# Chunk-selected attention with a gated MLP: scores of four pairs with 128-row contractions, k and q turned by TensorE, a new order

## The chip, the cores and the metric

The kernel runs on one core of one Trainium2 chip. Its time is the device time of one execution in microseconds (us). The core has five engines that run their own instruction streams and wait for each other by semaphores: TensorE (PE, matmuls and transposes), VectorE (DVE), ScalarE (ACT), GpSimd (POOL) and SyncE (SP), which in this kernel only issues DMAs. All loads, stores and DMA transposes go through SP's one queue.

## The reference

q, k and v have the shape (4 batches, 8 heads, 768 positions, 64). For every query a bound on its score with each chunk of 32 keys is made from the chunk's minimum and maximum, the six chunks with the highest bound among those that are not in the future are kept, and softmax attention runs over their keys alone, causally. The result goes through a gated MLP whose gate mixes positions.

```python
ub = sum(max(q * k_min, q * k_max))          # per query and chunk of 32 keys
ub = where(causal, ub, -1e9)
top = argsort(ub)[..., -6:]
scores = q @ k.T / 8                         # outside top or in the future: -1e9
attn = softmax(scores); x = attn @ v         # (4, 768, 512) after joining heads
h = relu(x @ w_in); u, v = h[:512], h[512:]
v_s = w_spatial @ normalised(v) + b_spatial  # mixes the 768 positions
out = (u * v_s) @ w_out
```

## The kernel before

Work is cut into 16 pairs of heads (pair i is batch i // 4, heads 2(i % 4) and the next one). The four pairs of batch 0 run in halves of 384 positions (tags `0a`, `0b` ...), the others whole (tags `4` to `15`). All work is on 16-bit floats; only the accumulators, loads and stores are 32 bits wide.

**How the order is set.** Every operation is an `Op` with a name, the engines that it may run on with a planned cost, its readers and writers. Nothing in the loops sets the order in time: `plan.replay(ORDER)` reads a long table, found by a search offline, word by word. `sc12_0P:10` says: operation `sc12_0` next, on engine P (P is PE, D is DVE, A is ACT, G is POOL, S is SP), its new buffers are number 1 and 0 of their rings. Each engine runs its own words in this order. The sizes of the rings stand in `RINGS` (L144); four matmul buffers `gen` (one PSUM bank each) and two `sc` (two banks each) are shared by all of PE's work. The planned costs stand in the functions `t_dve`, `t_act`, `t_pool`, `t_pe` (L27 to L40) and in the `op` calls; they matter to the search and not to the replay.

**Preparing a pair** (`load`, `prep`). k, q and v of the pair are loaded in 32 bits (`ld_`, L469 to L488): for v, and for k and q of pairs outside `PE_T` (pairs 10 to 15), each row of 64 numbers is one run of 256 bytes; for pairs in `PE_T`, six neighbouring rows go to one partition. `c_k`, `c_q`, `c_v` cast them (on POOL, DVE or ACT). To bring the 64 dimensions of both heads onto the 128 partitions, pairs in `PE_T` use six PE transposes (`t_k`, `t_q`, L516) and a copy out of PSUM (`e_k`, `e_q`, through `copy`, L302 to L306), and the other pairs one DMA transpose of k and q together (`x_kq`, L524). The result is a tile `kqT`. Then come the chunk maxima and negated minima (`kmm0`, `kmm1`, L530, DVE), their copy into a block layout for two heads (`km0`, `km1`), the rectified q and -q (`rq0`, `rq1`, L544 to L548), and the bounds on PE (`ub`, L558: for each of six tiles of 128 queries two matmuls of 48 columns, relu(q) with the maxima and relu(-q) with the negated minima). DVE adds the causal term to the diagonal chunks (`ubm`, L567), finds the six highest (`max`, L581), compares (`sel`, L602 or L605); `grd` (L590) writes a guard column. PE transposes the selection (`tsel`, L616, three transposes for a pair) and `es` copies it to the tile `selT`.

**Scores** (`attend`). A whole pair has three groups (`WHOLE`, L247), each with strips of key tile times query tiles in two buffers. For each strip and head a matmul of 64 rows gives q·k (L658; the two heads lie in rows 0 to 63 and 64 to 127), and a matmul of 32 rows adds the mask (L671: the selection times `expand`, a matrix of -30000 over each chunk). `exp` (ACT, L693) makes the weights, `tri` (POOL, L704) cuts the diagonal, `av` (PE, L727) multiplies with v and a column of ones, `rec` and `nrm` (DVE) divide, and `xx` (DMA, L748) or `tx` and `ex` turn the result for the MLP.

**The MLP of a batch** (`mlp`, called when the four pairs of the batch are done, its operations spread through the next batch's). Six v projections (`v`), their relu (`rv`), statistics (`bn`, `ag`), 1/sigma by two ACT operations (`ln`, `rs`), the normalisation (`vn`, L808, DVE), six u projections (`u`, `ru`), the mixing of positions (`s`, L826), the gate (`g`, L830, DVE), a DMA transpose (`xg`, L847), the output projection (`o`, L855), its eviction (`eo`) and the store (`so`, L860). Weights are loaded, cast and, for w_spatial, turned by PE (`tws`, `ews`). `WARM` are matmuls without use ahead of the first data (`w0` to `w3`, L424).

## Time and profile before

| | |
|---|---|
| median of three runs | 205.67 us (204.78 to 205.95) |
| the profiled execution's own time | 205.87 us |
| its span, first to last instruction | 204.0 us |
| mean granted clock of PE | 0.988 |
| busy: PE, DVE, ACT, POOL | 190.9, 164.5, 145.8, 80.1 us |
| bytes moved by DMA | 38.28 MB in 86989 packets, 74416 of them under 512 B |

In the lines that follow, a line of instruction groups names the source line, the engine, the operation, output and input tiles, shapes and the count, then busy time and mean duration, then the engine's idle time ahead of them and what ended it. A row of stretches has the stretch and its length, then the busy time of PE, PEld (weight loads), DVE, ACT and POOL with their numbers of instructions, then PE's granted clock, the mean busy share of the 16 DMA engines, and GB/s. A row of the chain has start, length, and what ran; the chain goes back from the last instruction to whatever released each step. A row of the timeline has start, length, engine, line, operation, tiles and count, and in brackets the idle time before it and what ended it.

### The profile page before, as it was taken

How to read it: one execution, taken by the hardware profiler on the slowest of the kernel's cores; microseconds unless marked ns; L12 is line 12 of the kernel's file. 1: busy time of each engine (PE TensorE's matmuls, PEld its weight loads, DVE VectorE, ACT ScalarE, POOL GpSimd, SP SyncE). 2: the span in 40 equal slices, each digit the busy share in tenths (PEclk: the TensorE clock that was granted, in tenths of full speed). 3: DMA queues.
4: the chain of work that ended last, by engine and by line, in shares of the span. 5: the costliest groups of instructions: out<-in, count | busy, mean ns of one | idle time of the engine just before them, and what ended most of it. 6: DMA issues, size and time to landing. Idle time of an engine off the chain costs nothing.

```text
span 204.0 us, 5938 instructions
## 1 busy us (share of the span) xinstructions
PE 190.9 (94%) x2282; PEld 103.3 (51%) x2282; DVE 164.5 (81%) x523; ACT 145.8 (71%) x232; POOL 80.1 (39%) x167
## 2 busy tenths in 40 slices
PE   7899989999998999798999999999999999999991
PEld 2456646576564455454355554544455456444440
DVE  2699999999999999798499896979998418894352
ACT  4689989999999498746797986687884673344221
POOL 5377848785795455631304642101451121000000
PEclk9969999999999999999999999999999999999998
DMA  5999999989999599699999869999200570701844
GB/s 167 278 249 292 287 359 280 319 223 310 275 208 238 92 224 236 142 145 263 236 213 230 155 78 262 148 261 224 40 0 3 132 154 5 204 2 51 206 156 157
DMA packets 86989, 38.28 MB, mean 188 GB/s; under 512 B 74416, under 2 KB 81584, under 8 KB 86960
## 3 DMA queue, kind: packets, MB, share of 16 engines
q1 hardware_dynamic: 86960, 37.89, 79.4%
q8 instruction: 18, 0.29, 0.6%
q14 instruction: 11, 0.09, 0.1%
HBM read 24.38 MB, written 6.29 MB: 150 GB/s over the span
## 4 chain that ended last, share of the span: by engine, by line
PE 59%; DVE 20%; DMA 7%; POOL 7%; issue 4%; ACT 2%; POOLq 0%; DVEq 0%; ACTq 0%
PE gen L776 16%; PE gen L826 11%; PE gen L855 7%; PE gen L727 7%; PE sc L658 6%; DVE kmm L530 5%; PE sc L671 4%; DMA st<-in_q_dram 3%; POOL n L306 3%; DMA late<-late 2%; PE sc L424 2%; DMA out_dram<-late 2%; DVE max L581 2%; DVE vn L808 2%; PE gen L616 2%
## 5 line engine op out<-in xcount | busy, mean ns | idle before, releaser
L693 ACT ACTIVATE e<-sc 128x768 f16<-128x768 f32 (+1 forms) x96 | 83.2, 917 | 23.3 <-PE sc L671 22.4
L704 POOL TENSOR_SCALAR_AFFINE_SELECT e<-e 128x512 f16<-128x512 f16 (+1 forms) x44 | 28.6, 662 | 31.8 <-ACT e L693 30.0
L826 PE MATMUL gen<-vn,wsT 128*128 128x512 f16 x144 | 34.4, 380 | 0.0
L530 DVE TENSOR_REDUCE kmm<-kqT 128x24 f16<-128x768 f16 (+1 forms) x40 | 30.7, 780 | 0.4 <-ACT kqT L304 0.2
L658 PE MATMUL sc<-kqT 64*128 64x128 f16 (+2 forms) x344 | 27.4, 272 | 0.3 <-ACT e L693 0.3
L727 PE MATMUL gen<-vt,e 128*128 128x65 f16 x672 | 24.8, 193 | 0.5 <-DVE selT L306 0.3
L727 PEld LDWEIGHTS <-e 128*128 128x128 f16 x672 | 23.0, 97 | 4.5 <-issue 1.6
L855 PE MATMUL gen<-w_out,late 128*128 128x512 f16 x96 | 23.7, 379 | 1.2 <-DMA late<-late 1.2
L830 DVE SCALAR_TENSOR_TENSOR late<-gen,bcol,u 128x512 f16<-128x512 f32 x24 | 17.7, 745 | 7.8 <-PE gen L826 7.8
L826 PEld LDWEIGHTS <-wsT 128*128 128x128 f16 x144 | 12.9, 98 | 15.7 <-issue 2.6
L671 PE MATMUL sc<-selT,expand 32*128 32x128 f16 (+2 forms) x344 | 19.0, 273 | 0.2 <-DVE selT L306 0.2
L658 PEld LDWEIGHTS <-kqT 64*128 64x128 f16 x344 | 11.8, 94 | 13.5 <-issue 9.8
L304 ACT ACTIVATE kqT<-gen 128x384 f16<-128x384 f16 (+1 forms) x24 | 15.0, 640 | 3.9 <-PE gen L516 3.7
L794 DVE BATCH_NORM_STATS2 stats<-vraw 128x6 f32<-128x512 f32 x24 | 15.8, 679 | 0.8 <-ACT vraw L783 0.8
L783 ACT ACTIVATE vraw<-gen 128x512 f32<-128x512 f32 x19 | 11.0, 607 | 6.7 <-PE gen L776 6.7
L306 POOL COPY km<-kmm 64x48 f16<-64x48 f16 (+1 forms) x27 | 6.6, 248 | 23.3 <-DVE kmm L530 19.6
L304 ACT ACTIVATE late<-gen 128x512 f32<-128x512 f32 (+1 forms) x12 | 7.1, 598 | 11.4 <-PE gen L839 5.3
L306 DVE COPY late<-gen 128x512 f32<-128x512 f32 x14 | 9.4, 687 | 7.1 <-PE gen L855 5.5
L581 DVE MAX8 max<-gen 128x8 f32<-128x20 f32 (+4 forms) x160 | 14.8, 164 | 0.1
L306 POOL CAST n<-st 128x768 f16<-128x768 f32 x17 | 13.9, 832 | 2.1 <-DMA st<-in_q_dram 1.6
L776 PEld LDWEIGHTS <-early 128*128 128x128 f16 x96 | 9.0, 98 | 11.0 <-issue 0.8
L783 ACT ACTIVATE u<-gen 128x512 f16<-128x512 f32 x18 | 10.5, 601 | 5.5 <-PE gen L776 5.5
(102 smaller groups left out, 299.3 us busy)
## 6 DMA issues: line engine op xcount, KB each, us to landing
out_dram<-late SPq DMA_DIRECT2D x24, 256.0 KB, 2.6
st<-in_q_dram SPq DMA_DIRECT2D x12, 384.0 KB, 5.8
st<-in_k_dram SPq DMA_DIRECT2D x12, 384.0 KB, 5.4
st<-in_v_dram SPq DMA_DIRECT2D x12, 384.0 KB, 6.1
st<-in_moe_w_spatial_dram SPq DMA_DIRECT2D x6, 384.0 KB, 5.1
st<-in_moe_w_in_dram SPq DMA_DIRECT2D x8, 256.0 KB, 4.4
early<-in_k_dram SPq DMA_DIRECT2D x8, 192.0 KB, 3.4
early<-in_q_dram SPq DMA_DIRECT2D x8, 192.0 KB, 3.7
```

The costliest lines, as they stand in the source:

```text
L304: e.activation(out=out, in_=in_, func=Act.Copy)
L306: e.tensor_copy(out, in_)
L530: lambda e, m=m, f=f: e.tensor_reduce(kmm.t[:, m, 0:nch], kq.t[:, 0, s0:s0 + ns].rearrange("d (c j) -> d c j", j=CHUNK), axis=AX.X, op=f, ...
L658: e.matmul(sc[z].t[:, a:a + len(qs) * P].rearrange("p (t c) -> p t c", c=P), lhsT=kq.t[r, 0, t * P:(t + 1) * P], rhs=qv[r, qs[0]:qs[-1] + ...
L671: e.matmul(sc[z].t[:, a:a + len(qs) * P], lhsT=expand.t[r, t * P:(t + 1) * P], rhs=selT.t[r].rearrange("p z c -> p (z c)")[:, c0:c0 + len( ...
L693: e.activation(out=e_.t[:, z, :, 0:w], in_=x.t.rearrange("p (h c) -> p h c", h=2)[:, :, 0:w], func=Act.Exp, scale=scale)
L704: e.affine_select(out=d, in_=d, compare_op=Alu.is_ge, fill=0.0, base=0, channel_multiplier=-1, pattern=[[0, 2 * len(zs)], [1, P]])
L727: e.matmul(avv()[:, n, hi, :], lhsT=es[g].t[:, zz, hi, c:c + P], rhs=vt.t[:, t, hi, 0:D + 1], start=(t == 0), stop=(t == qi))
L776: e.matmul(acc.t, lhsT=x.t[:, ko, t * P:(t + 1) * P], rhs=w.t[:, ko, :], start=(ko == 0), stop=(ko == NDO - 1))
L783: e.activation(dst.t, acc.t, func=Act.Relu)
L826: e.matmul(acc.t, lhsT=wsT.t[:, s, t * P:(t + 1) * P], rhs=vn[s].t, start=(s == 0), stop=(s == NQT - 1))
L855: e.matmul(acc.t, lhsT=gT.t[:, a2 * KO + ko, :], rhs=w_out.t[:, ko, :], start=(ko == 0), stop=(ko == KO - 1))
```

## The change

- **Wide scores.** For pairs 12 to 15 (`WIDE`) one matmul of 128 rows replaces the two of 64 and 32. Its stationary tile `kw` has, for head 0, k in rows 0 to 63 and `expand` in rows 64 to 127, and for head 1 the other way round; k is copied there by `kw0` and `kw1`. Its moving tile `qw` has q and the selection of a head below each other: `c_s` copies q beside the selection in a tile `qs`, `sel` and `grd` write into the same tile, and the DMA transpose `xs` (SP) turns all of it. `tsel` and `es` of these pairs are gone.
- **Turning k and q.** `PE_T` is now pairs 0 to 11. In pairs 12 to 15 (`K_T`) k is turned by PE and loaded in the form of `PE_T`, and q by a DMA transpose of its own (`x_q`). `x_kq` and its ring `kq16` are gone.
- **Bounds.** In pairs 0 to 5 (`UB3`) the bound is three matmuls, q with the maxima, relu(-q) with the maxima, relu(-q) with the negated minima, so that `rq0` is gone, and the causal term is a fourth small matmul (`tri` with the new tile `first`), so that `ubm` is gone.
- **The normalisation** is scale and shift: a new small DVE operation `sh` makes -mean/sigma, and `vn` may run on ACT, which six of the 24 do.
- **Order, rings and planned costs.** `ORDER` is new throughout; `st` has 9 buffers, `n16` 6; the tiles lie in a different order in memory, after a tile of 64 columns that nothing uses. Planned costs of casts, `ub`, `grd`, `rq`, `w` and DMA transposes differ. `FOLDS` is 0, so its loop does nothing.

```diff
-PE_T = range(10)
+PE_T = range(12)
...
+UB3 = range(6)
+WIDE = range(12, 16)
+K_T = range(12, 16)
...
-            runs = n != "v" and i in PE_T
+            runs = n != "v" and i in PE_T or n == "k" and i in K_T
...
+            if wide and nm == "q":
+                qs = buf("qs")
+                op(f"c_s{tag}", {"POOL": t_pool(ns), "DVE": 267.0, "ACT": t_act(ns) + 40.0},
+                   lambda e, nat=nat: copy(e, within(qs.t, 0, D), nat.t if both is None else nat.t[:, 1]),
+                   reads=[nat if both is None else (nat, nm)], writes=[(qs, "q")])
+            if i in K_T and nm == "q":
+                op(f"x_q{tag}", {"SP": XBAR},
+                   lambda e, nat=nat: e.dma_start_transpose(out=kq.t[:, 1].rearrange("p (t c) -> p t c", c=P),
+                                                            in_=nat.t.rearrange("p t h d -> p (t h d)")),
+                   reads=[nat], writes=[(kq, ("q", half))], dma=("x", S))
+                continue
...
+        if wide:
+            kw = st["kw"] = buf("kw")
+            for hi in range(2):
+                r = slice(hi * D, (hi + 1) * D)
+                op(f"kw{hi}_{tag}", {"POOL": t_pool(ns), "DVE": 267.0, "ACT": t_act(ns) + 40.0},
+                   lambda e, hi=hi, r=r: copy(e, kw.t[r, hi], kq.t[r, 0]), reads=[(kq, ("k", half))], writes=[(kw, hi)])
...
-        for m, sign in ((0, 1.0), (1, -1.0)):
+        three = i in UB3
+        for m, sign in ((1, -1.0),) if three else ((0, 1.0), (1, -1.0)):
...
-                for m in range(2):
+                terms = ((kq.t[:, 1, s0:s0 + ns], 0), (rq.t[:, 1], 0), (rq.t[:, 1], 1)) if three else ((rq.t[:, 0], 0), (rq.t[:, 1], 1))
+                for n, (x, m) in enumerate(terms):
...
+                if causal:
+                    e.matmul(ub.t[:, z * W:(z + 1) * W].rearrange("p (s c) -> p s c", c=NCH)[:, :, CPT * t:CPT * (t + 1)],
+                             lhsT=tri.t, rhs=first.t, start=False, stop=True)
...
+        if wide:
+            qw = st["qw"] = buf("kqT")
+            op(f"xs{tag}", {"SP": XBAR + 200.0},
+               lambda e: e.dma_start_transpose(out=qw.t.rearrange("p n (t c) -> p (n t) c", c=P), in_=qs.t),
+               reads=[qs], writes=[qw], dma=("x", 2 * S))
...
+            def go_wide(e, sc=sc, laid=laid):
+                qv = st["qw"].t.rearrange("p n s -> p (n s)").rearrange("p (t h c) -> p h t c", h=2, c=P)
+                for z in range(2):
+                    for s, (t, qs, col) in enumerate(laid[z][0]):
+                        for hi in range(2):
+                            a = hi * BANK + col
+                            e.matmul(sc[z].t[:, a:a + len(qs) * P].rearrange("p (t c) -> p t c", c=P),
+                                     lhsT=st["kw"].t[:, hi, t * P:(t + 1) * P], rhs=qv[:, hi, qs[0]:qs[-1] + 1:step],
+                                     start=(s == 0), stop=True, skip_group_check=True)
...
+                op(f"sh{b}_{h}", {"DVE": 100.0},
+                   lambda e, h=h: e.scalar_tensor_tensor(rstd[h].t[:, 1], in0=mv[h].t[:, :, 0:1], scalar=-1.0,
+                                                         in1=rstd[h].t[:, 0], op0=Alu.mult, op1=Alu.mult),
+                   reads=[mv[h], (rstd[h], 0)], writes=[(rstd[h], 1)])
...
+                        if e is nc.scalar:
+                            e.activation(vn[t2].t, vraw[t2].t, func=Act.Identity, scale=rstd[h].t[:, 0, r2], bias=rstd[h].t[:, 1, r2])
```

Some of the new order, around the first two wide pairs:

```diff
+nrm9_1D: g1_4D:0 g1_3D:1 xs12S:5 s1_5P:1 o1_1P:3 sc11_1P:01 rq1_14A: so1_0S: so0_5S: xx9S:0 g1_5D: kmm0_13D:0
+kmm1_13D: s1_2P:0 av10_1P:2 g1_2D: xg1_5S:0 exp11_11A:2 exp11_10A: eo1_1A:0 km1_13A:1 km0_13A: sc12_0P:10 tri11_20G:
...
+km0_15G:4 grd13G: km1_15G: x_q15S: v2_0P:2 rq1_15A:0 bn2_1D:2 rq0_15D: so1_3S: xs13S:0 sc13_2P:10 rv2_0A:1 exp13_20A:6
```

387 lines of the change are left out of this document (220 added, 167 removed).

## The prediction

> **What bounds the kernel now.** I read the page's shares first, then busy time by stretches cut at TensorE's own landmarks (`sc0b_0` starts at 23.5, `sc4_0` at 47.1, `sc6_0` at 67.8, `sc8_0` at 87.4, the last matmul ends at 199.7), then the chain that ended last, then single engines.
>
> ```profile
> span 204.0 us, 5938 instructions
> PE 190.9 (94%) x2282; PEld 103.3 (51%) x2282; DVE 164.5 (81%) x523; ACT 145.8 (71%) x232; POOL 80.1 (39%) x167
> ...
> PE 59%; DVE 20%; DMA 7%; POOL 7%; issue 4%; ACT 2%; POOLq 0%; DVEq 0%; ACTq 0%
> ```
>
> TensorE (PE) is busy 94% of the span, but a mean says nothing about where it could have been more.
>
> ```profile
> 0.00:23.50 23.50, 20.21 (x226) 12.02 (x228) 17.17 (x79) 18.17 (x38) 14.39 (x47) 0.93 0.88 252
> 23.50:47.10 23.60, 22.41 (x354) 14.14 (x352) 22.68 (x80) 22.00 (x31) 17.66 (x36) 1.00 0.97 298
> 47.10:67.80 20.70, 19.42 (x269) 10.88 (x269) 20.41 (x63) 19.24 (x31) 14.60 (x24) 1.00 1.04 236
> 67.80:87.40 19.60, 18.24 (x277) 10.36 (x278) 17.89 (x58) 14.82 (x21) 10.67 (x21) 1.00 0.98 184
> 87.40:107.40 20.00, 18.77 (x228) 9.59 (x226) 16.16 (x56) 14.86 (x24) 4.34 (x11) 1.00 1.15 215
> 107.40:199.70 92.30, 91.86 (x945) 46.35 (x941) 69.75 (x195) 56.16 (x89) 18.44 (x32) 1.00 0.58 127
> ```
>
> There are two kernels in this one. From 107.4 to 199.7 PE is busy 91.86 of 92.30 us: here the time is the sum of PE's work, and nothing else. From 23.5 to 67.8 VectorE (DVE) is busy 22.68 + 20.41 = 43.09 of 44.3 us, ScalarE (ACT) 41.24, and the DMA engines stand at 0.97 to 1.04: PE shows 41.83, but its busy time counts the latency of short matmuls that wait on each other, so what sets this stretch is DVE, with ACT and the DMA engines close behind. Between the two lies a stretch with waits (67.8 to 107.4). So I price the change as PE work after `sc8_0`, and as a balance of engines before it.
>
> **The wide scores (pairs 12 to 15).** Before, a group of a pair's scores is a run of 64-row matmuls, two heads side by side, and a run of 32-row mask matmuls:
>
> ```profile
> 160.03 0.49 PE sc L658 x8
> 160.51 0.33 PE sc L671 x8
> 160.84 1.40 PE gen L826 x6
> ...
> 171.82 0.67 PE gen L759 x12
> ...
> 184.57 5.18 PE gen L826 x24
> ```
>
> The last row is 24 matmuls of 512 columns in 5.18 us, 0.216 us each. One group costs 0.49 + 0.33, and the six 512-column matmuls behind it 1.40 instead of 6 x 0.216 = 1.29: 0.11 more, the change of row layout. That is 0.92 us. After, a group is 14 blocks of 128 columns on all 128 rows (seven blocks, two heads): 1792 columns at 0.216 us per 512 are 0.76 us, without a change of layout. Twelve groups save 12 x 0.16 = 1.9 us. The selection's transposes of these pairs go too: the row of 12 transposes in 0.67 us makes 0.056 us of one, so 4 x 3 x 0.056 = 0.7 us. Both lie in the PE-bound stretch and count in full: **-2.6 us**.
>
> A rule speaks against this part. The Trainium skill, "TensorE: Matmul & The Clock Gate", section "Why this matters for your kernels", advises to put contractions under 128 rows into separate row groups, so that they run concurrently; widening them to 128 rows does the opposite. By that rule alone the change would lose here (the last rival below). The rows above do not bear it out: 0.82 us and 0.11 more where full concurrency would make 0.59; "TensorEngine Tiling (Array Packing)", section "Key Properties", says that a change of tiling mode drains the engine, which fits the 0.11.
>
> **Turned by TensorE instead of DMA.** k of pairs 10 to 15 and q of 10 and 11 are eight times six transposes: 48 x 0.056 = 2.7 us of PE. Two of the eight (`t_k13`, `t_k15`) stand behind `sc8_0` in the new order: +0.7 us there, +2.0 ahead of it.
>
> **The causal term and the third matmul (pairs 0 to 5).** Twelve bound matmuls start 0.30 us before the next operation:
>
> ```profile
> 139.78 0.46 PE L558 MATMUL gen<-km,rq 128*128 128x48 f16 x12
> 140.08 1.02 PE L776 MATMUL gen<-w_u,xT 128*128 128x512 f16 x4
> ```
>
> so 0.025 us each; 36 tiles x 2 more = 72, **+1.8 us** of PE, all ahead of `sc6_0`, where DVE sets the pace. There it takes work from DVE, priced next.
>
> **DVE, ACT and POOL ahead of `sc8_0`.** I counted the words of both orders up to `sc8_0` and priced them by these rows (busy over count):
>
> ```profile
> L530 DVE TENSOR_REDUCE kmm<-kqT 128x24 f16<-128x768 f16 x24 | 22.3, 936 | 0.1
> ...
> L306 DVE COPY selT<-gen 128x384 f16<-128x384 f16 x15 | 5.3, 351 | 1.8 <-PE gen L616 1.8
> ...
> L546 DVE TENSOR_SCALAR rq<-kqT 128x768 f16<-128x768 f16 x9 | 3.7, 414 | 0.0
> ...
> L567 DVE TENSOR_TENSOR gen<-gen,cmask 128x48 f32<-128x48 f32 x12 | 2.4, 203 | 0.5 <-PE gen L558 0.5
> ...
> L306 DVE COPY kqT<-gen 128x768 f16<-128x768 f16 x1 | 0.9, 950 | 0.0
> ```
>
> Removed: 10 causal additions (0.20 each: 2.0 us), 8 rectified q (0.41 each: 3.3) and 4 copies of selT (0.35 each: 1.4). Added: 3 chunk reductions, moved ahead (0.93 each: 2.8), and 4 evictions of turned k and q, three whole (0.95) and one half of that (3.3). The rest goes both ways (guards, casts and evictions that change places with POOL and ACT, small constants) and nets to about +3.2 by the means of its groups. In all 9.3 - 6.7, **+2.6 us on DVE**. The same count gives about +5.8 on ACT and -8 on POOL; ACT has 87.4 - 74.2 = 13.2 us idle in the four rows above and can take it, though not between 23.5 and 67.8, where it had 3.1.
>
> What can hide 2.6 us of DVE: its idle time from 67.8 to 87.4 (19.60 - 17.89 = 1.7 us), which came from a late load:
>
> ```profile
> 77.20 6.00 DMA st<-in_q_dram
> 83.25 0.82 POOL kq L306
> ...
> 87.49 5.00 DMA late<-late
> ```
>
> One q load took 6.00 us to land, POOL's cast of it and the guard behind that ran late, and PE's transposes waited (1.36 us below). The change reads k of pairs 10 to 15 and q of 10 and 11 in runs of 1.5 KB instead of 256 B, a sixth of the packets, and moves these loads ahead. The rest, 0.9 us, I take from waits of DVE on POOL:
>
> ```profile
> L808 DVE TENSOR_SCALAR vn<-vraw,mv,rstd x24: 517/536/1162, 53.9 to 183.6; 128x512 f16<-128x512 f32 x24
> ```
>
> The same instruction takes 517 to 1162 ns. With 8 us less on POOL and the casts placed anew, a share of that spread (0.65 us on one operation) may come back; 0.9 us is a choice between 0 and 3.2 (five such operations), nearer to 0 because the median, 536, is near the minimum. The Trainium skill, "SBUF — State Buffer", section "SBUF: two separate sides", describes an exclusive lock between VectorE's two-port operations and GpSimd, which the spread agrees with; no row here shows the lock itself. So `sc8_0` **stays at 87.4**. Bounds: +3.8, if all of PE's 2.0 + 1.8 us there finds no gap and nothing of DVE's comes back; -3, if half of DVE's 6.3 idle us in the first 23.5 is used, where the new order starts `sc0a_0` with fewer operations ahead of it.
>
> **New and vanished waits behind `sc8_0`.**
>
> ```profile
> 86.08 0.34 PE L616 MATMUL gen<-ident,sn 128*128 128x128 f16 x3 [1.36 <-POOL sn L590]
> ...
> 92.54 1.90 PE L855 MATMUL gen<-w_out,late 128*128 128x512 f16 x8 [1.23 <-DMA late<-late]
> ```
>
> The second row is PE waiting 1.23 us for the DMA transpose of g that took 5.00 us to land, where the median of its kind is 3.3 (row below) and where the DMA engines stand at 1.15, the highest of the table. The change takes the six wide transposes of k and q out of the queue there (four of half the width remain) and a part of the small packets, so I take the wait as gone (-1.2; at worst 0). In its place stands `xs`: the selection now passes through the DMA queue.
>
> ```profile
> late<-late SPq DMA_TRANSPOSE x11, 3.3
> kqT<-kq SPq DMA_TRANSPOSE x6, 4.2
> ```
>
> For pair 13, PE has 9.6 us of work between `ub13` and `sc13_2` (0.8 + 0.3 + 0.8 + three of 0.86 + six of 0.86 by the chain's rows); the bound's maxima, comparison and guard need some 2.2, the DMA 4.2: it fits if SP's queue is free. For pair 15 the copy `c_s15` comes after `rec13_0`, and PE has 5.7 us until `sc15_0`, against 0.4 for the copy and 4.2 to landing: a margin of 1.1 that `xg2_1`, ahead of it in the queue, can use up. A late `xs` also holds back `xg`, `xx` and the stores queued behind it on SP. I take 0.4 us for all four, between 0 and 4 (1 us each). The shift sum `sh` (8 small DVE operations) and six `vn` on ACT lie beside the u projections, five of 0.86 us.
>
> **The tail.**
>
> ```profile
> 197.82 1.89 PE L855 MATMUL gen<-w_out,late 128*128 128x512 f16 x8
> ```
>
> ```profile
> 200.09 0.60 ACT L304 ACTIVATE late<-gen 128x512 f32<-128x512 f32 x1 [1.47 <-DMA out_dram<-late]
> ```
>
> PE ends at 199.71, ACT's last eviction starts at 200.09, because its buffer was still being stored. The new order gives the last eviction the buffer of `eo3_2`, stored first among the last four: between 0 and -0.4, I take -0.3.
>
> **The sum**, against the profiled execution's own 205.87 us (span 204.0 and 1.87 around it): 205.87 + 0 - 2.6 + 0.7 - 1.2 + 0.4 - 0.3 = 202.9 us. That execution lies 0.2 above the median of the three runs (205.67), so **202.7 us**, 1.4% faster.
>
> **The rivals.**
> *The front gives it back (slower).* Between 23.5 and 67.8 DVE has 1.2 us to spare and ACT 3.1; the change puts more on both and 3.8 us on PE. If nothing of it finds cover, `sc8_0` starts at 91.2, and 202.7 + 3.8 = 206.5; with the 1.23 us wait not gone, 207.7. I write 207. It decides from a start of `sc8_0` later than 90.4, where the 3.0 us won behind it are spent. For it: every engine but POOL gets more work. Against it: the loads get cheaper and DVE's idle time there had a cause that the change removes.
> *The selection's DMA is late (no change).* About 0.55 us at each `xs` in place of 0.1, and the wait for g's transpose still there: 202.7 + 1.8 + 1.2 = 205.7. For it: 4.2 us to landing against 0.3 for three transposes on PE, and pair 15's thin margin. Against it: PE has 9.6 us for pair 13, and all those before it have bounds ready early.
> *The front gains (much faster).* `sc8_0` 3 us earlier: 199.7. For it: DVE idles 6.3 us in the first 23.5. Against it: these are mostly the first loads.
> *The wide scores don't save.* If the heads' row groups already ran side by side without loss, the 896 data and 512 mask columns of a group would be 0.59 us and the wide group 0.17 more: 12 x 0.17 = +2.0 in place of -1.9, 206.6. The measured 0.92 us speaks against it.
>
> **Chances.** Forecast 0.45, front slower 0.24, late selection 0.12, front gains 0.16, wide scores dearer 0.03. About 0.5% (1 us) is what a measurement of this kernel can tell from no change. Faster: the forecast (201 to 204.5 by itself) but for 0.04, and the front's gain: 0.57. Same: those 0.04 and most of the late selection: 0.13. Slower: the rest, 0.30. Range 198.5 to 207.5: it holds all cases but the ends of the first and third rival.
>
> **What would show it.** Score groups of pairs 12 to 15 at 0.76 us, without 0.11 behind them; no PE gap above 0.3 us behind a transpose named `qs`; `sc8_0` at 87.4 or before; PE without gaps from there to the end, some 2 us sooner after `sc8_0` than the 116.6 of before; `vn` and casts nearer their minimum. Wrong it would be with `sc8_0` past 90, or gaps of PE that a DMA from `qs` ends.

## The result, and the profile after

The changed kernel takes 209.27 us (median of four runs, 207.75 to 209.52) against 205.81 us for the kernel before in the same series; the ratio is 1.0126, 95% interval 1.0081 to 1.0172. It is slower by 1.3%, where 1.4% faster was predicted. (The two medians alone would make 1.7%: of the four runs of the kernel before one, in a slower state that its runs fall into now and then, took 208.85 us, so that the size of the loss is less sure than its sign.) Its profiled execution took 209.33 us with a span of 207.6.

Where the time went shows best in the starts of the same score groups, in us. The last column is the final experiment, told below.

| | before | after | difference | a_mend_ub3 |
|---|---|---|---|---|
| `sc0b_0` | 23.48 | 25.22 | +1.74 | 25.28 |
| `sc4_0` | 47.14 | 50.07 | +2.93 | 49.32 |
| `sc5_0` | 56.80 | 62.48 | +5.68 | 60.14 |
| `sc6_0` | 67.78 | 73.35 | +5.57 | 70.94 |
| `sc8_0` | 87.38 | 91.57 | +4.19 | 89.31 |
| end of the last matmul | 199.7 | 203.7 | +4.0 | 198.7 |
| span | 204.0 | 207.6 | +3.6 | 202.3 |

The page of the profile after (shares of the span, then the chain that ended last):

```profile
span 207.6 us, 6017 instructions
PE 192.0 (92%) x2302; PEld 109.2 (53%) x2302; DVE 170.8 (82%) x523; ACT 154.5 (74%) x244; POOL 86.1 (41%) x166
...
PE 50%; DVE 34%; ACT 5%; issue 5%; DMA 3%; POOL 2%; DVEq 0%; POOLq 0%; ACTq 0%
```

VectorE has 6.3 us more work than before, although the change took ten `rq` and ten `ubm` off it, and the chain runs through VectorE for 34% of the span, where it was 20%. The stretches, cut at `sc0b_0`, `sc4_0`, `sc6_0`, `sc8_0`, `sc10_0`, `sc12_0`, `sc14_0` and the last matmul:

```profile
0.00:25.22 25.22, 20.52 (x269) 12.45 (x269) 19.09 (x82) 20.67 (x43) 12.15 (x45) 1.00 0.90 272
25.22:50.07 24.85, 23.63 (x388) 14.96 (x387) 23.54 (x70) 23.03 (x32) 17.01 (x31) 1.00 1.06 360
50.07:73.35 23.28, 20.71 (x285) 11.82 (x283) 23.10 (x67) 19.98 (x34) 13.38 (x22) 1.00 0.52 139
73.35:91.57 18.22, 17.87 (x277) 10.31 (x276) 18.12 (x66) 16.71 (x24) 11.50 (x19) 1.00 0.94 203
91.57:113.80 22.23, 22.02 (x254) 11.35 (x254) 21.67 (x68) 19.64 (x32) 12.65 (x22) 1.00 0.98 228
113.80:133.25 19.45, 18.33 (x236) 9.70 (x235) 15.07 (x39) 13.94 (x19) 7.34 (x12) 1.00 0.47 111
133.25:157.21 23.96, 22.98 (x238) 13.63 (x235) 22.89 (x80) 17.46 (x29) 6.71 (x13) 1.00 0.41 92
157.21:203.70 46.49, 45.93 (x378) 24.95 (x374) 27.31 (x59) 22.45 (x36) 5.33 (x9) 1.00 0.45 118
```

From 50.07 to 73.35 VectorE is busy 23.10 of 23.28 us and TensorE only 20.71: 2.6 us of TensorE are lost there, where the row of before (47.10 to 67.80) had 1.3. From 73.35 on TensorE has little idle time, but VectorE is as full as TensorE from 91.57 to 113.80 and from 133.25 to 157.21. The prediction treated everything behind `sc8_0` as TensorE's sum alone.

Ahead of `sc8_0` TensorE is busy for 82.7 us and idle for 8.8 (the first four rows). Before it was busy for 80.3 and idle for 7.1, by the rows in the prediction. So 2.5 of the 4.2 us lost there are more busy time of TensorE itself, and 1.7 are more idle time. Up to `sc0b_0` it is nearly all idle time (+1.4), from there to `sc4_0` all busy time (+1.2), and from `sc4_0` to `sc6_0` half of each (+1.3 and +1.3); from `sc6_0` to `sc8_0` 1.0 us of idle time and 0.4 of busy time are won back. Busy time holds the modelled ends of the matmuls, so this is a count and not an exact split. b0_oldnorm below, nearly the kernel before and at a granted clock of 1.00 where the first row of before has 0.93, is busy for 79.5 us there, so the added busy time may be up to 3.2 us.

TensorE's waits behind `sc8_0`, summed by what ended them (us in total, times, longest):

```profile
PE gen L918 <- DVE selT L312: 1.0, 1, 1.0
PE gen L918 <- DVE vn L902: 1.0, 1, 1.0
PE gen L947 <- DMA late<-late: 0.6, 1, 0.6
```

That and smaller gaps make 2.87 us of idle time behind `sc8_0` (the last four rows above, length less TensorE's busy time), against 1.67 before by the same count. The wait of 1.23 us for a transpose of g is gone (one of 0.55 us has come in the last batch); two waits on VectorE stand in its place.

Where `sc5_0` loses 2.75 us more than `sc4_0`, the timeline of VectorE, of GpSimd and of TensorE shows one event:

```profile
50.62 2.25 DVE L603 TENSOR_SCALAR rq<-kqT 128x768 f16<-128x768 f16 x2
52.79 0.54 DVE L824 TENSOR_TENSOR x<-gen,rec 128x384 f16<-128x384 f32 x1
```

```profile
50.43 0.68 POOL L312 COPY km<-kmm 64x48 f16<-64x48 f16 x3
51.06 1.59 POOL L312 CAST n<-st 128x768 f16<-128x768 f32 x2
```

```profile
53.38 0.28 PE L845 MATMUL gen<-ident,x 128*128 128x128 f16 x2 [1.25 <-DVE x L824]
```

Two rectified q took 2.25 us. In the kernel before, two of them one behind the other took 0.62 us:

```profile
56.28 0.62 DVE L548 TENSOR_SCALAR rq<-kqT 128x768 f16<-128x768 f16 x2
```

After, they began 0.2 us into a run of five GpSimd instructions, whose only gap is one of 0.06 us ahead of the third copy. The first of the two took 0.42 us; the second took 1.91 us and ended 0.22 us behind the run (51.06 + 1.59 = 52.65). TensorE waited 1.25 us for the normalised x behind them on VectorE. The means moved the same way: the `rq` of whole pairs on VectorE took 652 ns over 15 of them after and 390 ns over 19 before. With those of the halves it is 10.1 us for 17 after and 10.6 us for 27 before, so that ten `rq` fewer saved VectorE 0.5 us.

The wide score groups are there, and as long as predicted. Narrow, before, and wide, after:

```profile
128.92 0.56 PE L658 MATMUL sc<-kqT 64*128 64x384 f16 x6
129.40 0.40 PE L671 MATMUL sc<-selT,expand 32*128 32x384 f16 x6
129.73 1.44 PE L727 MATMUL gen<-vt,e 128*128 128x65 f16 x42
```

```profile
133.25 0.92 PE L765 MATMUL sc<-kqT,early 128*128 128x384 f16 x6
134.01 1.98 PE L813 MATMUL gen<-vt,e 128*128 128x65 f16 x60
```

From the start of a group to the start of the next operation it is 0.81 us before (129.73 - 128.92) and 0.76 after (134.01 - 133.25). Over the twelve groups these sum to 9.91 and 9.17 us.

### The profile page after: what moved, and what is told of

Same layout as the page of the kernel before. It is cut to its first block, busy times and chain, and to the rows that moved or that the text cites. A ratio compares the mean times of both kernels' runs of the same rounds, so it can differ in the third digit from the quotient of the medians.

```text
span 207.6 us, 6017 instructions
## 1 busy us (share of the span) xinstructions
PE 192.0 (92%) x2302; PEld 109.2 (53%) x2302; DVE 170.8 (82%) x523; ACT 154.5 (74%) x244; POOL 86.1 (41%) x166
## 4 chain that ended last, share of the span: by engine, by line
PE 50%; DVE 34%; ACT 5%; issue 5%; DMA 3%; POOL 2%; DVEq 0%; POOLq 0%; ACTq 0%
PE gen L918 12%; PE gen L862 8%; PE gen L947 7%; PE gen L813 6%; DVE kmm L585 6%; PE sc L730 4%; DVE stats L880 4%; DVE max L642 3%; PE sc L765 3%; PE sc L743 3%; ACT e L779 2%; PE gen L553 2%; DVE kqT L312 2%; DMA late<-late 2%; PE sc L445 2%
## 5 line engine op out<-in xcount | busy, mean ns | idle before, releaser
L779 ACT ACTIVATE e<-sc 128x1024 f16<-128x1024 f32 (+1 forms) x96 | 83.5, 917 | 19.2 <-PE sc L765 9.9
L312 POOL CAST n<-st 128x768 f16<-128x768 f32 x26 | 22.4, 879 | 3.2 <-DMA st<-in_k_dram 2.3
L730 PE MATMUL sc<-kqT 64*128 64x128 f16 (+2 forms) x256 | 20.1, 270 | 0.0
L310 ACT ACTIVATE kqT<-gen 128x768 f16<-128x768 f16 (+1 forms) x26 | 16.9, 671 | 3.1 <-PE gen L553 3.1
L553 PE MATMUL gen<-ident,n 128*128 128x128 f16 x168 | 14.7, 219 | 2.0 <-DVE n L312 0.9
L310 ACT ACTIVATE late<-gen 128x512 f32<-128x512 f32 x17 | 10.2, 597 | 7.0 <-PE gen L947 7.0
L743 PE MATMUL sc<-selT,expand 32*128 32x128 f16 (+2 forms) x256 | 14.1, 272 | 0.0
L730 PEld LDWEIGHTS <-kqT 64*128 64x128 f16 x256 | 8.7, 94 | 9.9 <-issue 6.8
L553 PEld LDWEIGHTS <-n 128*128 128x128 f16 x168 | 10.6, 98 | 5.7 <-issue 1.5
L862 PEld LDWEIGHTS <-xT 128*128 128x128 f16 x96 | 8.6, 97 | 9.3 <-DVE kqT L312 0.5
```

Of the source, the lines that this page charges most:

```text
L310: e.activation(out=out, in_=in_, func=Act.Copy)
L312: e.tensor_copy(out, in_)
L553: e.transpose(o[:, t * P:(t + 1) * P], nat.t[:, t].rearrange("p h d -> p (h d)"), ident.t)
L730: e.matmul(sc[z].t[:, a:a + len(qs) * P].rearrange("p (t c) -> p t c", c=P), lhsT=kq.t[r, 0, t * P:(t + 1) * P], rhs=qv[r, qs[0]:qs[-1] + ...
L779: e.activation(out=e_.t[:, z, :, 0:w], in_=x.t.rearrange("p (h c) -> p h c", h=2)[:, :, 0:w], func=Act.Exp, scale=scale)
L862: e.matmul(acc.t, lhsT=x.t[:, ko, t * P:(t + 1) * P], rhs=w.t[:, ko, :], start=(ko == 0), stop=(ko == NDO - 1))
```

## The experiments

Each ratio is to the kernel before on the same chip, whose medians were 206.6 to 206.9 us in these series. Names beginning with `a_` alter the changed kernel, those with `b` go back to the order of before, and `pre_small` alters the kernel before. No run has the turning of k and q by TensorE alone, so that what this part of the change costs ahead of `sc8_0` is not shown.

One term is used throughout. *Two-port instructions* are here VectorE's copies, casts and `tensor_scalar` (`rq`, `vn`, `grd`) from one SBUF tile to another: the kinds that in these traces take much longer at some places than at others.

### The old order with the parts of the change

**b0_old_order** has the changed program, but `ORDER` of before with the eight `sh` (each behind its `rs`) and `first` put in, and all parts off: what is left of the change is the new normalisation, `first` and the layout of memory.

```diff
-UB3 = range(6)
-WIDE = range(12, 16)
-K_T = range(12, 16)
-PE_T = range(12)
+UB3 = ()
+WIDE = ()
+K_T = ()
+PE_T = range(10)
```

> The changed program with the order of before and its parts off (no wide scores, no third bound matmul, k and q of pairs 10 to 15 turned by DMA); left over are the scale-and-shift normalisation with its 8 small operations and the new places of the tiles in memory. If the parts and the order made the loss, this runs like before, 205.8 within 1 us. If the memory layout or the 8 operations ahead of the normalisation did, it is 1 us or more slower.

Measured: 208.94 us, ratio 1.0104 (1.0066 to 1.0142): slower by 2.1 us with none of the three main edits in it. `sc8_0` starts at 90.88.

**b_ub3** puts the third bound matmul and the causal one for pairs 0 to 5 on top.

```diff
+UB3 = range(6)
```

> As b0_old_order, with the third bound matmul and the causal matmul of pairs 0 to 5, whose rq0 and ubm words are dropped. Theory 'PE work finds no cover': +1 to +2 us on b0_old_order (72 matmuls of 0.025 us). Theory 'DVE sets the front': 10 causal additions (2.0 us) and 6 rectified q of DVE (2.5 us) less ahead of sc6_0, so -1 to -4 us, and sc6_0 that much earlier.

Measured: 208.01 us, 1.0072 (1.0026 to 1.0118), by the ratios 0.7 us below b0_old_order, which is within the two errors. Neither the loss of 1 to 2 us nor the gain of 1 to 4 us that the two theories wanted is shown.

**b0_oldnorm** takes the new normalisation out of b0_old_order.

```diff
-op0=Alu.mult, op1=Alu.add)          # x * (1/sigma) + sh
+op0=Alu.subtract, op1=Alu.mult)     # (x - mean) * (1/sigma), no sh
```

> b0_old_order with the kernel before's normalisation (subtract, then multiply; the eight sh gone), so that only the memory layout and the instruction first are left of the change. Theory A (sh and the new form of vn cost b0_old_order its 2.1 us): 206.3, sc8_0 at 88.3. Theory C (layout, or the later start through first, which is 1 us at sc0a_0, shifts every later VectorE instruction against GpSimd's runs): 208 to 209, sc8_0 at 90 or later.

Measured: 204.86 us, 0.9897 (0.9852 to 0.9942), `sc8_0` at 87.54. Eight instructions of 0.26 us in the mean, and the other form of `vn` (median 543 ns with `sh`, 539 without), cost 4.1 us. Without them this kernel beats the one before, with only layout and `first` different; why is open. Of the 3.3 us between the two traces at `sc8_0`, 0.5 are there ahead of the first `sh`. Another 0.95 come between 54 and 62 us, where behind `sh0_0` a `vn` takes 1.00 us in place of 0.54 and an `rq` 0.78 in place of 0.35. The largest part, 1.9 us, comes at one instruction, `rq0_9`: 0.38 us from 82.03 on here, 2.67 us from 83.48 on in b0_old_order. The same thing happened once more without `sh`, in b_onwide2 (below), whose order has the same 608 words as b0_oldnorm up to there. First VectorE, then GpSimd of b0_oldnorm:

```profile
82.03 0.38 DVE L601 TENSOR_SCALAR rq<-kqT 128x768 f16<-128x768 f16 x1
```

```profile
81.57 0.63 POOL L790 TENSOR_SCALAR_AFFINE_SELECT e<-e 128x512 f16<-128x512 f16 x1
83.08 0.82 POOL L312 CAST kq<-st 128x768 f16<-128x768 f32 x1 [0.88 <-DMA st<-in_q_dram]
```

The same of b_onwide2, and TensorE behind it:

```profile
82.13 2.67 DVE L602 TENSOR_SCALAR rq<-kqT 128x768 f16<-128x768 f16 x1
```

```profile
81.68 0.63 POOL L791 TENSOR_SCALAR_AFFINE_SELECT e<-e 128x512 f16<-128x512 f16 x1
82.26 0.82 POOL L313 CAST kq<-st 128x768 f16<-128x768 f32 x1
83.02 0.82 POOL L313 CAST vt<-st 128x768 f16<-128x768 f32 x1
83.80 0.63 POOL L791 TENSOR_SCALAR_AFFINE_SELECT e<-e 128x512 f16<-128x512 f16 x1
84.41 0.55 POOL L649 TENSOR_SCALAR sn<-max 128x12 f16<-128x12 f32 x1
```

```profile
86.34 0.70 PE L814 MATMUL gen<-vt,e 128*128 128x65 f16 x18 [1.94 <-DVE vt L313]
```

The `rq` starts 0.10 us later. What differs is that in b_onwide2 the q load has landed, and GpSimd's cast of it follows on the instruction before it at 82.26 without a gap, where b0_oldnorm had 0.88 us of waiting for the load. The `rq` waits through three more instructions, until GpSimd turns to the small `grd` at 84.41, and TensorE waits 1.94 us for the cast of v behind it. A load that landed in time made this stretch slower: `sc8_0` starts at 88.85, against 87.54.

**b0_mv** keeps `sh` and gives `rq0_9` and the two casts behind it to ScalarE.

```diff
-rq0_9D: g0_5D c_v6D:0 eo0_2D:2 ... c_v7D:5
+rq0_9A: g0_5D c_v6A:0 eo0_2D:2 ... c_v7A:5
```

> b0_old_order (208.9 us, with sh) with three VectorE instructions given to ScalarE: rq0_9, which took 2.67 us from 83.48 on in GpSimd's run of 83.0 to 86.8, and the casts c_v6 and c_v7 behind it, which would run into the same run. Theory A (undoing sh gave 4 us because that rq then ran ahead of the run, 0.38 us): sc8_0 falls from 90.9 to 88 to 89 and the time to 206.3 to 207.3. If sh costs by its own place and not through this run: sc8_0 at 90 or later, 208 or more.

Measured: 211.11 us, 1.0202 (1.0127 to 1.0276), `sc8_0` at 92.20. A miss: VectorE is free of the stall, but ScalarE does its words in order and comes to the casts at 87.58, behind two exponentials and the `rq`:

```profile
88.52 0.71 PE L814 MATMUL gen<-vt,e 128*128 128x65 f16 x10 [3.30 <-ACT vt L311]
```

So this run doesn't test the claim; it put a longer wait in place of the stall.

### The wide scores in the old order

**b_wide** is b0_old_order with the wide scores of pairs 12 to 15, their copies and presets on GpSimd; **b_onwide** is b0_oldnorm with them, copies on VectorE and ScalarE; **b_onwide2** is b_onwide with `xs12` moved behind `xg1_3` and most of VectorE's copies on GpSimd.

```diff
-WIDE = ()
+WIDE = range(12, 16)
...
-grd12D: ... x_kq14S:2 xg1_1S:1 ... xg1_3S:0
+grd12D: xs12S: ... x_kq14S:2 xg1_1S:1 ... xg1_3S:0    # b_onwide
+grd12D: ... x_kq14S:2 xg1_1S:1 ... xg1_3S:0 xs12S:    # b_onwide2
```

> As b0_old_order, with wide scores in pairs 12 to 15 (k and q still turned together by DMA). Theory 'PE-bound stretch counts its work': -2.6 us (twelve groups 0.16 less, twelve transposes less). Rival 'xs is late': PE gaps of 1 to 3 us ahead of sc13_0, whose selection is ready some 5 us before it, and no gain. Third: the copies c_s and kw on POOL slow DVE's two-port operations; then DVE busy grows by over 1 us behind 107 us.

> b0_oldnorm (204.9 us) with the wide scores of pairs 12 to 15 alone: the presets of qs on GpSimd behind 92 us, all copies for kw and qs on ScalarE and VectorE, k and q of these pairs still turned by DMA. Prediction's term (0.92 us a group becomes 0.76, and the transposes of the selection go): -2.6, 202.3. By the starts of the operations in the two traces (0.82 becomes 0.77): -0.7 and -0.7, 203.5. If the added copies (16 of 0.35 to 0.8 us and the presets) or the DMA of xs hold TensorE up: 205 or more, with gaps of TensorE at the sc of pairs 12 to 15.

> b_onwide (208.4 us) with its two losses taken out: xs12 goes behind xg1_3 in SyncE's queue (there it held xg1_1 back by 3.1 us and TensorE waited 2.45 us), and VectorE's copies for kw and qs of pairs 13 to 15 go to GpSimd, the presets of kw to ScalarE behind 100 us. If the wide scores save what their starts show (12 x 0.05) and the transposes of the selection (0.7): 203.5 to 204.3, against 204.9 without them. If the extra transposes in SyncE's queue or the copies still hold TensorE up: 205 or more, with TensorE's gaps at the sc or at w_out of pairs 11 to 15.

Measured: 218.38 us, 1.0572 (1.0494 to 1.065); 208.39 us, 1.0127 (1.0072 to 1.0183); 211.08 us, 1.0188 (1.0126 to 1.0249). All lose. In b_wide TensorE waits for GpSimd, whose presets and copies stand ahead of work that is due: 3.2 us for `km` (1.2 in b0_old_order), 3.1 us for exponentials cut by `tri`, 1.4 us for `sn`; it also waits 2.1 us for a transpose of g. In b_onwide SyncE's queue shows the largest loss (start, time to issue, what), then TensorE:

```profile
119.37 2.45 SPq L676 DMA_TRANSPOSE kqT<-snab  x1
121.99 1.40 SPq L562 DMA_TRANSPOSE kqT<-kq  x1
123.48 2.62 SPq L940 DMA_TRANSPOSE late<-late  x2
```

```profile
126.58 1.04 PE L948 MATMUL gen<-w_out,late 128*128 128x512 f16 x4 [2.45 <-DMA late<-late]
```

In b0_oldnorm the two transposes of g are issued from 120.36 on. Here `xs12` and the transpose behind it take their turn first (2.45 and 1.40 us to issue), g follows at 123.48, and TensorE waits 2.45 us. In b_onwide2 that wait is 0.52 us, but one of 1.53 us for a later g follows at 140.81, and the stall at 82.13 comes on top. A wide group without a gap behind it takes 0.76 to 0.77 us in all of them, against 0.82 for a narrow one. What the old order makes of the wide scores depends on where their 12 copies, four presets and four DMA transposes go; all three placements lose more by waits than the groups save, so that no run shows a gain of the whole kernel by the wide scores.

### GpSimd's casts

**a_split** halves GpSimd's casts of whole pairs, so that each instruction is shorter.

```diff
-copy(e, x, raw)
+for half in (0, 1):
+    copy(e, x[half], raw[half])                # GpSimd only
```

> The changed kernel, with POOL's casts of whole pairs and of w_spatial cut into two instructions each. Theory 'DVE waits for whole POOL instructions': the wait of a rectified q on DVE (0.35 us alone, 0.61 to 0.71 in the mean of the changed kernel) halves, the kernel gains 1 to 2 us, though POOL has some 35 instructions more. Rival 'the port does not matter': rq as slow as before the cut, time the same or up to 1 us slower.

Measured: 209.26 us, 1.0127 (1.007 to 1.0183), as the changed kernel. The stall is as long with four short casts as with two long ones (VectorE, then GpSimd):

```profile
50.37 2.50 DVE L608 TENSOR_SCALAR rq<-kqT 128x768 f16<-128x768 f16 x2
```

```profile
50.81 1.85 POOL L314 CAST n<-st 128x384 f16<-128x384 f32 x4
```

What counts is the run without a gap, not the length of one instruction in it.

**a_small** and **pre_small** cut those casts of GpSimd whose buffer has been filled once to 64 columns, in the changed kernel and in the kernel before. The rest of such a buffer keeps the values of an earlier pair, so the two kernels leave out a part of the work and are there for their time alone.

```diff
+if e is nc.gpsimd and old:
+    out, in_ = out[:, 0:1, 0:1], in_[:, 0:1, 0:1]
 copy(e, out, in_)
```

> The kernel before, with 19 of GpSimd's 58 casts (those whose buffer has been filled once already) cut to 64 of 768 columns, so the values of later pairs are stale: GpSimd's share of the shared-port time shrinks, nothing else changes. Theory A (the waits of VectorE's two-port instructions for GpSimd's back-to-back runs set the time in the stretch ahead of sc8_0): I put these waits at 5.4 us in the kernel before; about a third goes, and the time falls by about 1 us, to 204.8. Theory B (VectorE's own work, not the waits, sets that stretch): within 0.5 us of the kernel before, 205.8.

> The changed kernel, with 24 of GpSimd's 52 casts cut to 64 of 768 columns, the same rule (later pairs get stale values). Theory A: the waits, which I put at 10.0 us, fall by a third to a half, the mean of the whole-pair rq falls from 0.61 us towards 0.4, sc8_0 starts 2 us or more ahead of 91.57, and the time falls by 2 to 3.5 us, to 206 to 207.3; it falls by more than in the kernel before. Theory B: the rq get shorter, but sc8_0 stays within 1 us of 91.57 and the time within 1 us of 209.3.

Measured: pre_small 204.55 us, 0.9889 (0.9839 to 0.9939), some 2.2 us less than the kernel before; a_small 205.50 us, 0.9938 (0.9915 to 0.9962), 3.8 us less than the changed kernel, with `sc8_0` at 88.47 in place of 91.57. The difference between the two kernels shrinks, by the ratios from 1.3% to 0.5%. But the two runs gain in different ways, and theory A holds for one of them at most. I add up, for every two-port instruction ahead of 92 us, what it takes beyond the shortest of its kind and shape. In a_small this falls from 8.1 us to 5.1. TensorE's wait of 1.25 us for VectorE at 53.38 is gone, and its idle time ahead of `sc8_0` falls from 8.8 us to 6.4. In pre_small it does not fall (3.5 us in the kernel before, 3.9 here). What goes there are TensorE's own waits for GpSimd, first before, then pre_small:

```profile
PE gen L616 <- POOL sn L590: 2.0, 2, 1.4
```

```profile
PE gen L627 <- POOL sn L601: 0.6, 1, 0.6
```

GpSimd finishes earlier with shorter casts in a_small too, and 24 casts were cut there against 19, so how much of a_small's 3.8 us is VectorE's waiting isn't separated here.

### The stall at 50.6 us, and other single edits of the changed kernel

**a_mv** moves the two `rq` to where GpSimd is idle, and the cast `c_v3b` behind them.

```diff
-e_q5D: ... c_v3bD: ... rec2bD:2 rec1bD:0 nrm1bD:1 rq1_6D:0 rq1_5D:1 ... ex1bD:
+e_q5D: rq1_6D:0 rq1_5D:1 ... rec2bD:2 rec1bD:0 nrm1bD:1 ... ex1bD: c_v3bD:
```

> The changed kernel with three VectorE instructions moved in the order, nothing else: rq1_6 and rq1_5 go from behind nrm1b to right behind e_q5 (49.4 us, while GpSimd is idle), and the cast c_v3b goes from ahead of rec2b to behind ex1b. Theory A (a two-port instruction of VectorE that starts in a back-to-back run of GpSimd waits for the run's end; here two rq took 2.25 us from 50.62 on, in GpSimd's run of 50.43 to 52.65): the rq take 0.3 us each, sc4_1 starts 1.2 to 1.6 us earlier than 54.76, and the time falls to 207.5 to 208.3. Theory B (the 2.25 us are VectorE's work or another wait): sc4_1 within 0.3 us, the time within 0.5 us of 209.3.

Measured: 210.00 us, 1.0186 (1.015 to 1.0222): 0.7 us slower still. VectorE, then TensorE:

```profile
49.62 0.62 DVE L605 TENSOR_SCALAR rq<-kqT 128x768 f16<-128x768 f16 x2
...
51.75 1.30 DVE L314 CAST vt<-early 128x384 f16<-128x384 f32 x1
```

```profile
53.10 0.97 PE L815 MATMUL gen<-vt,e 128*128 128x65 f16 x27 [1.57 <-DVE vt L314]
```

The two `rq` take 0.31 us each, as expected. The cast that I put in their place is an instruction of the same kind, and the same run of GpSimd (50.64 to 52.84) held it: 1.30 us. The wait had only been passed on.

**a_mv3** gives that cast to ScalarE.

```diff
-ex1bD: c_v3bD:
+c_v3bA: exp4_01A:5
```

> a_mv mended: rq1_6 and rq1_5 behind e_q5 as there, and the cast c_v3b, which in a_mv ran into the same run of GpSimd (1.30 us, TensorE waiting 1.57 us for it), done by ScalarE ahead of exp4_01. VectorE then has no two-port instruction in GpSimd's run of 50.6 to 52.8. Theory A: TensorE's wait ahead of sc4_1 goes, sc4_1 at 53.2 to 53.7 in place of 54.76, and 1.0 to 1.5 us of it last to the end: 207.8 to 208.3. Theory D (the next wait, ScalarE's or a later run of GpSimd, takes the place of this one): sc4_1 earlier, sc6_0 within 0.4 us of 73.35 and the time within 0.5 us of 209.3.

Measured: 207.07 us, 1.0019 (0.9988 to 1.0051), level with the kernel before. VectorE, then TensorE:

```profile
49.35 0.61 DVE L605 TENSOR_SCALAR rq<-kqT 128x768 f16<-128x768 f16 x2
```

```profile
51.00 1.36 PE L815 MATMUL gen<-vt,e 128*128 128x65 f16 x30
...
53.56 0.56 PE L732 MATMUL sc<-kqT 64*128 64x256 f16 x8
```

`sc4_1` starts at 53.56 (54.76), `sc8_0` at 90.25 (91.57): three words of the order are worth 1.3 us at `sc8_0` and 2.2 us at the end, more than expected. TensorE's sums ahead of `sc8_0`:

```profile
sum 90.25, PE 82.91 PEld 49.68 DVE 82.01 ACT 80.17 POOL 53.77; mean PE 20.73 PEld 12.42 DVE 20.50 ACT 20.04 POOL 13.44
```

Its idle time there is 7.3 us in place of 8.8, near the 7.1 of before, and its busy time is that of the changed kernel. Most of the gain behind `sc8_0` lies in the last batch, where the wait for a g of 0.55 us doesn't come; it is 0 to 0.8 us in the profiled executions of the kernels that share the order there.

**a_oldnorm** takes the new normalisation out of the changed kernel, the edit of b0_oldnorm, with all `vn` on VectorE; **a_ub3_10** sets `UB3 = range(10)`, and four `rq0` and four `ubm` go; **a_combo** is a_mv with both.

> The changed kernel with the kernel before's normalisation: the eight sh go (2.4 us of VectorE in all), and the six vn that ScalarE did go back to VectorE (6 x about 0.6 us). Theory S (sh costs time by itself, in every order, as undoing it gave 4 us in the old order): 206 to 207.5. Theory P (in the old order it cost by moving one rq into a run of GpSimd, and only there): VectorE's sum changes by about +1 us, and the time stays within 1 us of 209.3.

> The changed kernel with the third bound matmul and the causal one for pairs 6 to 9 as well: it takes four rq0 (0.61 us each) and four ubm (0.20 us) off VectorE ahead of sc10_0, 3.2 us, and adds 4 x 12 matmuls of 0.025 us, 1.2 us, to TensorE. Theory A and B alike (VectorE sets the stretch up to sc8_0, by its waits or its work): sc8_0 at 89 to 90.5, the time 207 to 208.3. Theory D (the order of TensorE or the loads set it, and VectorE only looks full): sc8_0 at 91.5 or later, the time 209.3 to 210.

> The changed kernel with the moves of a_mv, the old normalisation of a_oldnorm and the third bound matmul for pairs 6 to 9 as in a_ub3_10. If the three gains are separate (1.5, 0 to 1, 1.0): 206 to 207. If what bounds the stretch behind 73 us is TensorE itself, which shows no gap there in the changed kernel, the gains ahead of it still count in full, as they move its start. If the gains hide each other: 207.5 or more.

Measured: 207.96 us, 1.0077 (1.0044 to 1.011); 208.25 us, 1.0068 (1.0037 to 1.0098); 208.18 us, 1.0115 (1.007 to 1.0159). The normalisation costs 1.3 us here by the medians (1.0 by the ratios), a third or less of what it cost in the old order, although the edit also brings six `vn` back from ScalarE to VectorE. I read its price as that of the places where it moves others. a_ub3_10 took 3.2 us off VectorE ahead of `sc10_0`, and `sc8_0` came only 0.3 us earlier: the stall at 50.6 is that of `rq1_6` and `rq1_5`, which still took 2.24 us, and from 73 us on TensorE has no gap. In a_combo the cast `c_v3b` takes 1.30 us and TensorE waits 1.57 us for it, as in a_mv, which hides what the other two edits give ahead of it.

**a_now0** leaves out `w0`, nine matmuls on zeros that the new order puts at 11.97 us.

```diff
 for j, n in enumerate(WARM):
+    if not j:
+        continue
```

> The changed kernel without w0, nine matmuls on zeros that keep TensorE busy and which the new order puts at 11.97 us, 1.94 us long, ahead of the transposes for sc1a_0. If their place on TensorE made sc1a_0 late (16.24 against 14.97 before): sc1a_0 at 15.0 to 15.7 and the time down by 0.5 to 1. If VectorE's cast c_q2a behind them sets it (TensorE waits 0.90 us for it): sc1a_0 within 0.2 us. The kernel before had a granted clock of 0.86 in its stretch of 11 to 23 us, the changed one 1.00: if the nine matmuls bought that, the clock falls there and the stretch up to sc0b_0 is no shorter.

Measured: 209.62 us, 1.0156 (1.01 to 1.0213). Nothing won; the same stretch of a_now0 and of the changed kernel:

```profile
9.40:25.20 15.80, 12.99 (x205) 8.98 (x203) 14.17 (x61) 13.67 (x31) 7.52 (x27) 0.78 0.98 284
```

```profile
9.40:25.20 15.80, 13.75 (x225) 9.28 (x223) 15.03 (x64) 14.71 (x33) 8.65 (x30) 1.00 0.98 293
```

The granted clock (the column behind GpSimd's) falls to 0.78 and `sc0b_0` comes 1.3 us later. The nine matmuls pay for themselves; the 1.7 us of the first 25 us are not theirs.

### The change, mended

**a_mend** is a_mv3 with two more places altered, at TensorE's waits of 1.0 us; **a_mend_ub3** adds `UB3 = range(10)`.

```diff
-vn1_3D:0 c_v10D:1 vn1_1D:1 rq0_12D: vn1_5D:2 es11D:0
+vn1_3D:0 es11D:0 vn1_1D:1 vn1_5D:2 rq0_12D: c_v10D:1
...
-vn2_4A:4 ... vn2_0D:5 vn2_2D:0 vn2_3D:1 vn2_1D:2
+vn2_4A:4 vn2_1A:2 ... vn2_0D:5 vn2_2D:0 vn2_3D:1
```

> a_mv3 (207.1 us) with two more places mended, both of TensorE's waits of 1.0 us behind sc8_0. At 112 us VectorE's cast c_v10 (1.18 us in a run of GpSimd) goes behind vn1_1, vn1_5 and rq0_12, and es11 ahead of them, so that s1_0 gets its last vn earlier; at 149 us vn2_1 goes to ScalarE, so that s2_0 waits for three vn fewer than six on VectorE. If TensorE's waits there are what VectorE's lateness costs: about 0.6 and 0.5 us, 205.7 to 206.3, level with the kernel before (206.9 on the last chip) or just faster. If the stretches behind are set by VectorE's sum (21.67 of 22.23 us and 22.89 of 23.96): the waits come back later, 206.8 to 207.4.

> a_mend with the third bound matmul and the causal one for pairs 6 to 9 as well, which gave 1.0 us to the changed kernel (a_ub3_10) where the stall at 50.6 us stood in front of it. If that gain adds: 204.8 to 205.6. If TensorE, which has no gap from 73 to 91 us, sets the time there, its 1.2 us more of matmuls eat it: within 0.4 us of a_mend.

Measured: a_mend 205.70 us, 0.9946 (0.9913 to 0.9979); a_mend_ub3 204.72 us, 0.9893 (0.9849 to 0.9936), faster than both kernels by 2.2 and, by the ratios, some 4.8 us. TensorE in a_mend_ub3, summed over the stretches as above, first ahead of `sc8_0` (89.31), then from there to the last matmul:

```profile
sum 89.31, PE 82.81 PEld 50.84 DVE 78.64 ACT 80.17 POOL 53.09; mean PE 20.70 PEld 12.71 DVE 19.66 ACT 20.04 POOL 13.27
```

```profile
sum 109.37, PE 108.92 PEld 59.58 DVE 85.92 ACT 74.30 POOL 32.28; mean PE 27.23 PEld 14.89 DVE 21.48 ACT 18.57 POOL 8.07
```

It is 109.37 us from `sc8_0` to the end of the last matmul (198.68), against 112.33 before: 3.0 us less, where the prediction wanted 2.7 up to there and 0.3 behind it. So what it wanted behind `sc8_0` is reached when VectorE isn't late there. Ahead of `sc8_0` 1.9 us remain lost. TensorE's idle time there is 6.5 us, 0.6 less than before, and its busy time 2.5 us more, so what is left is by this count TensorE's added work, that for the bounds of pairs 6 to 9 included. The excess of the two-port instructions ahead of 92 us is 2.9 us here, against 3.5 before.

## Why the prediction was wrong

Its numbers went the way of its first rival, the front that gives it back: 91.2 and 206.5 to 207.7 were written there, 91.57 and 209.27 came. Its mechanism, TensorE's added work that finds no cover, holds for a part: 2.5 us more busy time came for the 3.8 it named. The other 1.7 us are idle time that it didn't have, so that 91.57 lies so near to 91.2 is in part luck. Of the 6.4 us between the forecast of 202.9 and the profiled execution's 209.33, 4.2 lie ahead of `sc8_0` and 2.5 between there and the last matmul, where 112.13 us came for the 109.6 that the terms make of 112.33.

*"`sc8_0` stays at 87.4"* failed, in two of its steps. One is that TensorE's 2.0 + 1.8 us of added work there were put at nothing, because VectorE sets the pace: 2.5 us of them show as busy time, and about as much is left in a_mv3 and a_mend_ub3, where the idle time is back to that of before or less. The other is *"the rest, 0.9 us, I take from waits of DVE on POOL ... may come back"*. By each two-port instruction's excess over the shortest of its kind, as I estimate it from the rows of VectorE's timeline, these waits were 3.5 us ahead of 92 us before and 8.1 after: +4.6 where -0.9 was booked. I counted GpSimd's busy time (8 us less) and took the waits to follow it. The count was wrong too: up to `sc8_0` the traces have 54.0 us of GpSimd after and 57.3 before, 3.3 less, and 83.9 us of VectorE after and 78.2 before, 5.7 more, where 2.6 less the 0.9 were booked. And the waits don't follow GpSimd's sum. They follow the coincidence of a run of GpSimd with a two-port instruction on VectorE, and a new order draws that lot anew. a_mv3 shows it: with two `rq` and a cast out of one such run, `sc8_0` comes 1.3 us earlier, the kernel 2.2. Their sum is not the loss, though: in a_ub3_10 it falls from 8.1 us to 5.1, and `sc8_0` comes 0.3 us earlier. What counts is the wait that TensorE's next work stands behind. The Trainium skill, "SBUF — State Buffer", section "SBUF: two separate sides", says that whichever side starts first holds the shared port for the whole instruction. The trace agrees that VectorE's instruction waits, and differs in how long: 2.67 us, through four instructions of GpSimd.

*The loss up to `sc0b_0` (+1.7) and from there to `sc4_0` (+1.2).* The second is busy time of TensorE (+1.2, with 34 matmuls more); the first is nearly all idle time, and what set it isn't settled. From `sc0b_0` to `sc4_0` a_mend takes 24.60 us and a_mend_ub3 24.04, two kernels with the same order up to there (24.85 after, 23.66 before), so half of the second can vary between executions; of the 1.7 us a_now0 only shows that the matmuls on zeros are not the cause.

*The wide scores, -1.9,* was mis-sized: -0.7 (9.91 us for the twelve groups less 9.17). I took "0.11 more, the change of row layout" from a chain row of 1.40 us for six matmuls. By the starts those six take 1.30 us in both kernels (160.78 to 162.08 before), so that no row shows the 0.11 for a change of row layout; the chain's rows end where the modelled end of the last matmul lies. The Trainium skill, "TensorE: Matmul & The Clock Gate", section "Single matmul latency", gives the latency of one matmul apart from the pitch of many, and by its formula 512 columns take 0.38 us; the trace has 379 ns in the mean for one, and 0.216 us from start to start. The rival "the wide scores don't save" didn't come true either: they save, somewhat over a third of what was written.

*-0.7 for `tsel`, +0.7 for `t_k13` and `t_k15`* hold: 12 transposes fewer and 12 more behind `sc8_0`, at 0.056 us.

*"Both lie in the PE-bound stretch and count in full"* failed. From 91.57 to 113.80 and from 133.25 to 157.21 VectorE is as full as TensorE, and waits of 1.0 us on it came at 117 and 153 us. I had read the stretch of before, 69.75 us of VectorE in 92.30, as one; one part of it was nearly full already:

```profile
128.92:149.90 20.98, 20.56 (x233) 9.96 (x233) 18.92 (x72) 16.46 (x27) 4.33 (x10) 1.00 0.76 151
```

a_mend takes the two waits away, and from `sc8_0` to `sc15_1` it takes 77.88 us where a_mv3 takes 79.89.

*The wait for g (-1.2)* went as predicted where it stood, but one of 0.55 us came in the last batch; `xs` (+0.4) cost nothing in the changed order; b_onwide shows what it costs in another (2.45 us). *The tail (-0.3)*: the span ends 3.9 us behind the last matmul, 4.3 before.

*`sh`: "lie beside the u projections"*, booked at nothing: with the new form of `vn` 1.3 us in the changed kernel, 4.1 in the old order.

## What to carry to other kernels

A replayed order is tuned to the phases between engines: 0.1 us at one instruction was worth 2.3 us at another, and eight instructions of 0.26 us, with a new form of another, were worth some 4 us. So price an edit at the place where it shifts two engines against each other, and look, on the path, for VectorE's copies, casts and `tensor_scalar` that start inside a run of GpSimd. When such a stall is mended, ask which instruction of the same kind moves up into the run. Take matmul pitches from starts in the timeline and not from the chain's durations, and don't call a stretch bound by one engine before cutting it finer. Where another engine seems to set the pace, work added to the engine with the most work is still not free: ask into which of its gaps it goes.

## What was not expected of the hardware

In these stalls a two-port instruction of VectorE did not get in between two back-to-back instructions of GpSimd: an `rq` that takes 0.38 us in b0_oldnorm took 2.67 us, through four of them, and the two of 0.62 us took 2.50 us with the casts cut in halves. With nine matmuls on zeros, 1.94 us long, the granted clock of the stretch from 9.4 to 25.2 us stood at 1.00; without them it was 0.78. The Trainium skill, "TensorE: Matmul & The Clock Gate", section "What's actually happening", describes such a gate that opens with sustained activity, and the trace agrees. `sh`, an instruction on 128 x 3 numbers, took 295 ns in the mean where 100 were planned: 130 to 155 ns in five of the eight, and 299, 554 and 774 ns in the others.
